# Reordered loads, unread products between the first scans, and a respread weight conversion in a fused SSD and MLP kernel

## The chip, the cores and the metric

The kernel runs on one core of a Trainium2 chip. The metric is the device time of one execution in microseconds (us). The core has a matmul engine (TensorE, PE in the tables, with its weight loads as PEld), a vector engine (VectorE, DVE), a scalar engine (ScalarE, ACT), GpSimd (POOL) and SyncE (SP), whose queue issues most of the transfers; ACT can issue transfers too. Each engine works through its own queue in order. Operands lie in SBUF, matmuls write to PSUM.

## The reference

Two stages follow each other. The first is a Mamba-2 state-space scan over 4 batches, 8 heads, 768 steps, head size 32 and state size 16. Written without its chunks of 32, with `a` clipped to 1e-6..1 and `cum` the running sum of log a:

```
L    = exp(cum[i] - cum[j]) for j <= i, else 0
y    = ((C B^T) * L) x  +  (C state) * exp(cum)
state = exp(sum log a) * state + sum_j exp(cum[-1] - cum[j]) B_j x_j
```

The second stage takes the 3072 tokens with their 8 x 32 values as 256 features:

```
h = x @ w_in            # 256 x 2048
g = h * sigmoid(1.702 h)
out = g @ w_out         # 2048 x 256
```

The weights are float64 in memory.

## The kernel before

**Tiling.** The 3072 tokens form six groups of 512 tokens. A group has two pairs `p` of 128-step chunks, so there are 12 pairs. For a group the scan stage leaves `yT`, then the hidden stage makes 16 tiles `h` (two matmuls each, over 256 features) that ACT turns into `gT` (line 402), then the projection adds up `o` over the 16 `gT`. For group 0 the projection runs in the order of the 16 blocks f (`project_all`, line 417), for the others by 128 tokens (`project`, line 410). A dictionary of places (`in_hidden[g][f]`, `in_project[g][f]`, lines 471 to 505) says which other work is written between two of these tiles. Nothing is rescheduled: `in_order` keeps each engine's instructions in the order in which the program was written.

**One pair of the scan.** `fan` (line 253): ACT copies the decay values `az` into `X`, four matmuls spread them over the partitions into PSUM `ab`. `decay_pair` (line 271): DVE makes the decay matrix `L` with four scans over `ab`. Later pairs (from 4 on) scan a tile `a` instead that a transfer has spread out of a scratch in DRAM (`spread`, line 175; `decay`, line 242). `ends` scales B to `Be`. `turn` transposes B and C (`tp`) and ACT copies them to `BT` and `CT`, DVE makes `CsT`. `scores` makes C B^T in PSUM `cb`, and DVE multiplies it into `L` (line 339). `advance` makes the new state `S` from `A` = Be^T x. `finish` adds up `y`, and ACT copies it to `yT`. `decay_rows` (line 292) clips and scans `af`, the decay values along the rows.

**Weights.** The float64 weights come as 16 pieces of 512 KB, 8 of `w_in` and 8 of `w_out`, each for two of the 16 blocks f. `fetch(i)` loads piece i as `bits`; `unpack(i)` starts with `fetch(i + AHEAD)` and then takes exponent and mantissa apart (ACT `m`, `z`, `p2`, DVE `e`, `u`); `narrow(i)` first does `unpack(i + 1)`, then three DVE steps that end in float32 weights. `bits` has AHEAD + 1 = 5 buffers, so a fetch waits until the piece five before it has been used.

**PSUM.** `h`, `o` and the first pair's `ab` share the two buffers of tag "ff"; the `ab` of other pairs shares one buffer with `cb`.

**Transfers.** All go out from SP in the order of the program, except piece 0 and x of the pairs 0 and 1, which ACT issues. Eight transfers of SP and ACT can be outstanding: each waits for the one that last used its completion counter. B and C of a pair are 64-byte runs, x 128-byte runs.

Of the kernel before, what the change touches and what calls it, by code (L numbers as in the profile page):

```python
# [8 lines left out]
FP32 = mybir.dt.float32  # L9
# [25 lines left out]
def kernel(  # L35
# [73 lines left out]
    AHEAD = 4  # L109
# [93 lines left out]

    early = const.tile([P, 1], FP32, name="early")
    nc.vector.memset(early, 0.0)
    nc.scalar.activation(early, early, AF.Silu)
    ident = const.tile([P, P], FP32, name="ident")
    make_identity(nc, ident)
    idents = const.tile([P, NH, P], FP32, name="idents")
    nc.gpsimd.tensor_copy(idents, ident.unsqueeze(1).to_broadcast([P, NH, P]))  # L210

# [5 lines left out]
    for r in range(R):  # L217
# [4 lines left out]


# [7 lines left out]
        fill=0.0, base=N - 1, channel_multiplier=-1)  # L231

# [38 lines left out]
    def decay_pair(p, ab):  # L271
# [3 lines left out]
        for r in range(R):  # L275
# [3 lines left out]
                initial=0.0, op0=ALU.mult, op1=ALU.add)  # L279

# [136 lines left out]
    def project_all(g, gT, between):  # L417
# [9 lines left out]
        for k in range(CG):  # L427
# [3 lines left out]
    nc.vector.tensor_scalar(out=az, in0=az, scalar1=1e-6, scalar2=1.0,  # L431
                            op0=ALU.max, op1=ALU.min)
    nc.vector.memset(az[:, :, 0:1], 0.0)
    for b in range(NB):
        nc.sync.dma_start(out=scratch[b].rearrange("c h s -> h c s"),
                          in_=az[b * NH:(b + 1) * NH])


    assert PG == 2
    decay_pair(0, fan(0, "ff"))  # L440
    second = fan(1, "cb")
    unpack(0)
# [4 lines left out]
    decay_pair(1, second)  # L447
    scores(0)
    advance(0)
    narrow(0)  # L450
# [8 lines left out]
    spread_rows(1)  # L459
    for p in range(PG, 2 * PG):  # L460
        load(p)
# [23 lines left out]

    for j in range(PG):
        p = PG + j
        at(in_hidden[0], 6 + 5 * j, lambda p=p: fan_at(p))
        at(in_hidden[0], 7 + 5 * j, lambda p=p: decay_at(p))
    for k, i in enumerate((8, 9, 10, 13, 14)):  # L490
        at(in_hidden[0], i, lambda k=k: narrow(NF // PF + k))
    for k, i in enumerate((2, 4, 6)):
        at(in_project[0], i, lambda k=k: narrow(NF // PF + 5 + k))
# [15 lines left out]
    for g in range(NG):  # L509
        if g + 2 < NG:  # L510
            for j in range(PG):
# [10 lines left out]
        if g + 2 < NG:  # L522
# [43 lines left out]
```

## Time and profile before

| | us |
|---|---|
| three runs, median (lowest to highest) | 457.79 (457.02 to 457.92) |
| profiled execution, time | 457.59 |
| profiled execution, span of its instructions | 455.6 |
| PE busy | 404.1 (89%) |
| DVE busy | 168.0 (37%) |
| ACT busy | 111.5 (24%) |

The span is what lies between the first and the last instruction; the execution is 2.0 us longer. Engines overlap, so busy times don't add up to the span. A busy PE is not a PE at its best rate: the clock of TensorE has two levels, 1.2 and 2.4 GHz, and the profile has a column with the granted share (0.50 or 1.00, or between where it changed inside a stretch). Work that belongs to the scan of group 0 ends at 45.0 us, its hidden stage at 103.4, its projection at 140.4, and the five other groups follow. In the rows, a matmul instruction on float32 operands shows as two records.

### The profile page before, as it was taken

How to read it: one execution, taken by the hardware profiler on the slowest of the kernel's cores; microseconds unless marked ns; L12 is line 12 of the kernel's file. 1: busy time of each engine (PE TensorE's matmuls, PEld its weight loads, DVE VectorE, ACT ScalarE, POOL GpSimd, SP SyncE). 2: the span in 40 equal slices, each digit the busy share in tenths (PEclk: the TensorE clock that was granted, in tenths of full speed). 3: DMA queues.
4: the chain of work that ended last, by engine and by line, in shares of the span. 5: the costliest groups of instructions: out<-in, count | busy, mean ns of one | idle time of the engine just before them, and what ended most of it. 6: DMA issues, size and time to landing. Idle time of an engine off the chain costs nothing.

```text
span 455.6 us, 4764 instructions
## 1 busy us (share of the span) xinstructions
PE 404.1 (89%) x1928; PEld 265.7 (58%) x1928; DVE 168.0 (37%) x227; ACT 111.5 (24%) x202; POOL 7.9 (2%) x27
## 2 busy tenths in 40 slices
PE   1547912789999999999999999999999999999996
PEld 0225300337885546885558875558855478844785
DVE  0876805977573640435051352202550300000000
ACT  3213805745202232002421012330023310033100
POOL 3000000000000000000000000000000000000000
PEclk9999975979999999999999999999999999999999
DMA  9801897260003920008600029100000000000000
GB/s 164 235 0 48 141 129 272 86 239 0 1 0 67 195 98 0 25 12 117 207 1 13 12 43 203 56 0 13 23 12 1 0 1 23 24 0 0 11 13 24
DMA packets 85973, 28.58 MB, mean 63 GB/s; under 512 B 75904, under 2 KB 79168, under 8 KB 85952
## 3 DMA queue, kind: packets, MB, share of 16 engines
q1 hardware_dynamic: 81520, 27.24, 25.4%
q10 hardware_dynamic: 4432, 1.05, 1.2%
q8 instruction: 15, 0.25, 0.2%
q14 instruction: 6, 0.05, 0.0%
HBM read 25.03 MB, written 3.24 MB: 62 GB/s over the span
## 4 chain that ended last, share of the span: by engine, by line
PE 80%; DVE 7%; SPq 5%; ACT 3%; DMA 2%; issue 2%; POOL 0%; ACTq 0%; DVEq 0%; POOLq 0%
PE h L399 31%; PE o L413 30%; PE o L424 6%; SPq L105 4%; DVE L L276 3%; PE cb L334 3%; PE y L386 3%; PE y L379 2%; PE ab L266 2%; PE A L349 2%; DMA b<-in_B_dram 1%; ACT z L146 1%; DMA bits<-in_moe_w_in_dram 1%; PE tp L313 1%; ACT p L147 1%
## 5 line engine op out<-in xcount | busy, mean ns | idle before, releaser
L399 PE MATMUL h<-yT,w_in 128*128 128x512 f32 x384 | 176.5, 605 | 2.8 <-ACT gT L402 1.5
L413 PE MATMUL o<-w_out,gT 128*128 128x256 f32 x640 | 138.9, 379 | 0.0
L413 PEld LDWEIGHTS o<-w_out,gT 128*128 128x128 f32 x640 | 121.6, 190 | 18.7 <-issue 2.4
L399 PEld LDWEIGHTS h<-yT,w_in 128*128 128x128 f32 x384 | 71.3, 192 | 86.6 <-issue 76.7
L402 ACT ACTIVATE gT<-h 128x512 f32<-128x512 f32 x96 | 57.1, 595 | 232.3 <-PE h L399 232.3
L406 DVE TENSOR_SCALAR ob<-o 128x256 f32<-128x256 f32 x24 | 10.1, 424 | 172.4 <-PE o L413 164.4
L266 PE MATMUL ab<-X,ones 32*128 32x512 f32 x32 | 11.1, 1126 | 32.4 <-ACT X L258 31.1
L248 DVE TENSOR_TENSOR_SCAN L<-a,idents 128x1024 f32<-128x1024 f32 x16 | 36.5, 2281 | 0.0
L339 DVE TENSOR_TENSOR L<-L,cb 128x2048 f32<-128x2048 f32 x12 | 27.4, 2287 | 17.6 <-PE cb L334 17.6
L424 PE MATMUL o<-w_out,gT 128*128 128x256 f32 x128 | 29.6, 383 | 0.8 <-ACT gT L402 0.8
L424 PEld LDWEIGHTS o<-w_out,gT 128*128 128x128 f32 x128 | 23.8, 190 | 5.2 <-ACT gT L402 1.2
L334 PE MATMUL cb<-CT,BT 32*128 32x256 f32 x192 | 15.6, 445 | 10.9 <-DVE L L276 7.4
L266 PEld LDWEIGHTS ab<-X,ones 32*128 32x128 f32 x32 | 3.5, 308 | 37.0 <-ACT X L258 32.8
L323 DVE TENSOR_TENSOR CsT<-tp,since 128x256 f32<-128x256 f32 (+1 forms) x12 | 4.5, 379 | 48.3 <-ACT CT L320 48.2
L276 DVE TENSOR_TENSOR_SCAN L<-ab,idents 128x512 f32<-128x512 f32 x16 | 18.4, 1204 | 10.1 <-PE ab L266 10.1
L334 PEld LDWEIGHTS cb<-CT,BT 32*128 32x128 f32 x192 | 9.8, 206 | 18.9 <-issue 14.5
L146 ACT ACTIVATE z<-e,edge 128x512 f32<-128x512 uint32 x16 | 11.5, 716 | 24.9 <-DVE e L142 24.9
L391 ACT ACTIVATE yT<-y 128x512 f32<-128x512 f32 x12 | 7.1, 595 | 30.5 <-PE y L386 30.5
L379 PEld LDWEIGHTS y<-CsT,S 128*128 128x128 f32 x80 | 11.2, 198 | 5.7 <-issue 4.5
L141 ACT ACTIVATE m<-bits 128x512 f32<-128x512 uint32 x16 | 10.7, 670 | 14.6 <-DMA bits<-in_moe_w_in_dram 13.4
L386 PE MATMUL y<-L,x 128*32 128x128 f32 x384 | 13.8, 287 | 0.0
L379 PE MATMUL y<-CsT,S 128*128 128x128 f32 x80 | 11.7, 285 | 0.9 <-DVE S L360 0.9
(47 smaller groups left out, 164.8 us busy)
## 6 DMA issues: line engine op xcount, KB each, us to landing
a<-scratch SPq DMA_DIRECT2D x16, 512.0 KB, 8.2
bits<-in_moe_w_out_dram SPq DMA_DIRECT2D x8, 512.0 KB, 3.5
bits<-in_moe_w_in_dram SPq DMA_DIRECT2D x7, 512.0 KB, 4.9
out_dram<-ob SPq DMA_DIRECT2D x24, 128.0 KB, 1.7
x<-in_x_dram SPq DMA_DIRECT2D x20, 128.0 KB, 2.9
b<-in_B_dram SPq DMA_DIRECT2D x24, 64.0 KB, 2.7
c<-in_C_dram SPq DMA_DIRECT2D x24, 64.0 KB, 2.6
af<-in_a_dram SPq DMA_DIRECT2D x4, 384.0 KB
```

What stands on the lines that cost most here:

```text
L105: queue.dma_start(out=dst[p][:, k], in_=src[b, :, sl, :].rearrange("h s d -> s h d"))
L248: nc.vector.tensor_tensor_scan(out=Ls[p][:, k].rearrange("p r q i -> p (r q i)"), data0=ra.pop(n), data1=idents.rearrange("p h i -> p (h i ...
L266: nc.tensor.matmul(out=ab[r], lhsT=ones[rows], rhs=X[rows].rearrange("p k q i -> p (k q i)"), start=True, stop=True, tile_position=(32 * r ...
L276: nc.vector.tensor_tensor_scan(out=L[:, r], data0=ab[r], data1=idents.rearrange("p h i -> p (h i)")[:, :2 * Q * P], initial=0.0, op0=ALU.m ...
L334: nc.tensor.matmul(out=cb[:, r, k], lhsT=BT[rows, k], rhs=CT[rows, k].rearrange("p q i -> p (q i)"), start=True, stop=True, tile_position= ...
L339: nc.vector.tensor_tensor(out=Lv, in0=Lv, in1=cb.rearrange("p r k e -> p k r e"), op=ALU.mult)
L379: nc.tensor.matmul(out=y[:, k, t], lhsT=old[:, t * P:(t + 1) * P], rhs=s["CsT"][:, k], start=first, stop=False, skip_group_check=True)
L386: nc.tensor.matmul(out=y[D * q:D * q + D, k, t], lhsT=rx[p][:, k, h], rhs=L[:, k, h // Q, h % Q], start=False, stop=True, tile_position=(0 ...
L399: nc.tensor.matmul(out=h, lhsT=w_in[:, k, f * P:(f + 1) * P], rhs=yT[g][:, k], start=(k == 0), stop=(k == NK - 1))
L402: nc.scalar.activation(gT, h, AF.Silu, scale=GELU_SCALE)
L413: nc.tensor.matmul(out=o, lhsT=gT[f][:, k * P:(k + 1) * P], rhs=w_out[:, f], start=(f == 0), stop=(f == NF - 1))
L424: nc.tensor.matmul(out=o[k // 2][:, k % 2], lhsT=gT[f][:, k * P:(k + 1) * P], rhs=w_out[:, f], start=(f == 0 and k % 2 == 0), stop=(f == N ...
```

## The change

- `AHEAD` is 6 and `bits` has 8 buffers. The tiles `a` of `spread` move from a ring of their own (4 buffers) into the ring of `bits`.
- The first transfers are put in another order: pieces 0 and 1 go out from SP behind `az`; then B and C of pair 0, `af`, all of pair 1, pieces 2 to 5, then all of the pairs 2 and 3, `af` of batch 1 and the scratch. ACT issues x of pair 0 alone, behind its table load. The pairs 4 and 5 and the tiles `a` of group 2 are loaded inside group 0's projection.
- POOL makes `pick` ahead of the identities. The clip of `az` is written earlier.
- `keep_busy` writes matmuls whose PSUM result `busy` is never read: three with ones ahead of the first `fan`, and one behind each of the eight scans of the pairs 0 and 1, which streams the scanned `L`.
- Piece 0 is unpacked before pair 1's `fan` and narrowed right behind pair 0's scans.
- The places in group 0: pieces 2 to 8 are narrowed in the hidden stage at f = 0, 1, 3, 4, 9, 10, 12, pieces 9 to 15 in the projection at 0, 2, 4, 6, 8, 10, 11. Before, pieces 2 to 12 were narrowed in the hidden stage and 13 to 15 in the projection. Other places shift by a few f.

```diff
-    AHEAD = 4
+    AHEAD = 6
-        bits[i] = t = wide.tile([P, 2 * PN], U32, tag="bits", name=f"bits{i}", bufs=AHEAD + 1)
+        bits[i] = t = wide.tile([P, 2 * PN], U32, tag="bits", name=f"bits{i}", bufs=AHEAD + 2)
...
-        ra[n] = raw.tile([P, NH * P], FP32, tag="a", name=f"a{n}", bufs=4)
+        ra[n] = wide.tile([P, NH * P], FP32, tag="bits", name=f"a{n}", bufs=AHEAD + 2)
...
-    fetch(0, nc.scalar)
+    fetch(0)
+    fetch(1)
+    early = const.tile([P, 1], FP32, name="early")
+    nc.vector.memset(early, 0.0)
+    nc.scalar.activation(early, early, AF.Silu)
     load(0, nc.scalar)
     spread_rows(0)
-    load(1, nc.scalar)
-    for i in range(1, AHEAD):
+    load(1)
+    for i in range(2, AHEAD):
         fetch(i)
+    for p in range(PG, 2 * PG):
+        load(p)
+    spread_rows(1)
...
+    busy = []
+    def keep_busy(rhs, n=1):
+        if not busy:
+            busy.append(ps.tile([P, 4 * P], FP32, tag="ff", name="busy"))
+        for i in range(n):
+            nc.tensor.matmul(out=busy[0], lhsT=ones, rhs=rhs, start=True, stop=True,
+                             skip_group_check=True)
...
-    def decay_pair(p, ab):
+    def decay_pair(p, ab, after=None):
...
+            if after:
+                after(L[:, r])
...
-    decay_pair(0, fan(0, "ff"))
+    keep_busy(ones.unsqueeze(1).to_broadcast([P, 4, P]), 3)
+    ab = fan(0, "ff")
+    unpack(0)
     second = fan(1, "cb")
-    unpack(0)
+    busy.clear()
+    decay_pair(0, ab, keep_busy)
+    narrow(0)
     decay_rows(0)
...
-    decay_pair(1, second)
+    decay_pair(1, second, keep_busy)
     scores(0)
     advance(0)
-    narrow(0)
     turn(1)
...
-    spread_rows(1)
-    for p in range(PG, 2 * PG):
-        load(p)
...
+    for i, k in zip((2, 3, 4, 5, 6, 7, 8), (0, 1, 3, 4, 9, 10, 12)):
+        at(in_hidden[0], k, lambda i=i: narrow(i))
+    for p, k in ((PG, 5), (PG + 1, 13)):
+        at(in_hidden[0], k, lambda p=p: fan_at(p))
+        at(in_hidden[0], k + 1, lambda p=p: decay_at(p))
+    for i, k in zip(range(9, 16), (0, 2, 4, 6, 8, 10, 11)):
+        at(in_project[0], k, lambda i=i: narrow(i))
+    for k in range(CG):
+        at(in_project[0], 3 + 2 * k, lambda k=k: spread(2 * CG + k))
+    for k in range(PG):
+        at(in_project[0], 4 + 4 * k, lambda k=k: load(2 * PG + k))
```

SP, from piece 6 on, before. The names are destination and source of a transfer (`bits6` is piece 6, `b2` is B of pair 2).

```order
L126 DMA bits6_291<-in_moe_w_in_dram 128x2x512
L186 DMA af1_328<-in_a_dram 128x1x768
L105 DMA b2_330<-in_B_dram 128x8x16 x2
L105 DMA c2_331<-in_C_dram 128x8x16 x2
L105 DMA x2_332<-in_x_dram 128x8x32 x2
L105 DMA b3_339<-in_B_dram 128x8x16 x2
L105 DMA c3_340<-in_C_dram 128x8x16 x2
L105 DMA x3_341<-in_x_dram 128x8x32 x2
L105 DMA b4_348<-in_B_dram 128x8x16 x2
L105 DMA c4_349<-in_C_dram 128x8x16 x2
L105 DMA x4_350<-in_x_dram 128x8x32 x2
```

B, C and x of pair 5 follow, and only then piece 7. SP, the same stretch now, from piece 5 on (`bits_116`; `bits_183`, `bits_213` and `bits_328` are the pieces 6, 7 and 8, `b_118` and `b_127` B of the pairs 2 and 3):

```order
L126 DMA bits_116<-in_moe_w_in_dram 128x2x512
L105 DMA b_118<-in_B_dram 128x8x16 x2
L105 DMA c_119<-in_C_dram 128x8x16 x2
L105 DMA x_120<-in_x_dram 128x8x32 x2
L105 DMA b_127<-in_B_dram 128x8x16 x2
L105 DMA c_128<-in_C_dram 128x8x16 x2
L105 DMA x_129<-in_x_dram 128x8x32 x2
L186 DMA af_136<-in_a_dram 128x1x768
L241 DMA scratch<-az 8x6x128 x4
L126 DMA bits_183<-in_moe_w_in_dram 128x2x512
L126 DMA bits_213<-in_moe_w_in_dram 128x2x512
L126 DMA bits_328<-in_moe_w_out_dram 128x2x512
```

Piece 7 stood behind 24 transfers of B, C and x that were issued after piece 6; now nothing stands between the two, and 12 such transfers and the scratch stand ahead of both.

PE in the first scans, before (`ab` of the pairs 0 and 1, the transposes `tp`, then `cb` and `A` of pair 0):

```order
L266 MATMUL ab_163<-X_160,ones 128x512 x4
L313 MATMUL tp_187<-ident,b_85 128x128 x2
L313 MATMUL tp_187<-ident,c_86 128x128 x2
L334 MATMUL cb_207<-CT_194,BT_192 128x256 x8
L349 MATMUL A_217<-x_87,Be_199 128x256 x2
```

And now:

```order
L278 MATMUL ab_198<-X_195,ones 128x512 x4
L290 MATMUL busy<-L_203,ones 128x512 x4
L337 MATMUL tp_235<-ident,b_90 128x128 x2
L337 MATMUL tp_235<-ident,c_91 128x128 x2
L290 MATMUL busy<-L_250,ones 128x512 x4
L358 MATMUL cb_259<-CT_242,BT_240 128x256 x8
L373 MATMUL A_269<-x_92,Be_247 128x256 x2
```

Four unread products stand ahead of the transposes of pair 0, four more ahead of its `cb`; each waits for its scan on DVE.

DVE between the scans of pair 0 and those of pair 1, before:

```order
L276 SCALAR_TENSOR_TENSOR L_155<-ab_3_150,idents 128x512
L142 TENSOR_SCALAR e_170<-bits_83 128x512
L148 TENSOR_SCALAR u_171<-bits_83 128x512
L295 TENSOR_SCALAR af_94<-af_94 128x768
L302 SCALAR_TENSOR_TENSOR since_185<-af_94,first_181 128x768
L323 TENSOR_TENSOR CsT_197<-tp_187,since_185 128x128
L286 TENSOR_TENSOR Be_199<-b_85,L_155 128x128 x2
L276 SCALAR_TENSOR_TENSOR L_202<-ab_163,idents 128x512 x4
```

And now:

```order
L298 SCALAR_TENSOR_TENSOR L_203<-ab_3_178,idents 128x512
L142 TENSOR_SCALAR e_215<-bits_85 128x512
L148 TENSOR_SCALAR u_216<-bits_85 128x512
L159 SCALAR_TENSOR_TENSOR m_187<-u_186,m_187 128x512
L161 SCALAR_TENSOR_TENSOR p_189<-bits_83,p_189 128x512
L167 TENSOR_TENSOR w_in<-m_187,p_189 128x2x256
L319 TENSOR_SCALAR af_99<-af_99 128x768
L326 SCALAR_TENSOR_TENSOR since_233<-af_99,first_229 128x768
L347 TENSOR_TENSOR CsT_245<-tp_235,since_233 128x128
L310 TENSOR_TENSOR Be_247<-b_90,L_203 128x128 x2
L298 SCALAR_TENSOR_TENSOR L_250<-ab_198,idents 128x512 x4
```

The whole of `narrow(0)`, with the unpacking of piece 1, now stands in front of `decay_rows`; the two steps on piece 0 went ahead of pair 0's scans, and the five steps leave the place behind pair 0's new state.

## Rows read from the trace of the kernel before

**Rows 1.** Stages: length, busy time per engine, granted clock, transfer share, GB/s

```profile
core 0: us, PE busy (x) PEld busy (x) DVE busy (x) ACT busy (x) POOL busy (x), PEclk, DMA share, GB/s
45.00:103.40 58.40, 35.55 (x84) 14.06 (x85) 37.04 (x66) 29.48 (x51) 0.00 (x0) 0.80 0.70 169
103.40:140.40 37.00, 36.17 (x249) 30.05 (x246) 24.00 (x32) 9.24 (x17) 1.04 (x3) 1.00 0.00 0
140.40:455.60 315.20, 311.18 (x1458) 208.88 (x1458) 80.03 (x89) 60.56 (x112) 1.34 (x5) 1.00 0.19 43
```

**Rows 2.** Timeline, the stall: start, us, engine, line, tiles, [idle before <- releaser]

```profile
45.62 1.93 SPq L105 DMA_DIRECT2D b<-in_B_dram  x2
...
66.52 0.53 SPq L126 DMA_DIRECT2D bits<-in_moe_w_in_dram  x1
...
70.67 0.43 DVE L142 TENSOR_SCALAR e<-bits 128x512 uint32<-128x512 uint32 x1 [13.96 <-DMA bits<-in_moe_w_in_dram]
...
76.77 2.09 PE L266 MATMUL ab<-X,ones 32*128 32x512 f32 x8 [17.45 <-ACT X L258]
```

**Rows 3.** Chain that ended last, up to 45 us: start, us, what

```profile
0.80 2.64 DMA az<-in_a_dram
...
7.76 0.57 DVE az L431
...
9.49 2.13 PE ab L266 x4
...
14.99 2.34 DVE L L276 x2
...
22.60 3.44 DVE L L276 x3
...
26.17 2.12 PE cb L334 x16
...
28.32 2.29 DVE L L339
...
31.25 0.48 DVE S L360
...
34.69 2.09 PE cb L334 x16
...
40.82 0.70 DVE S L353
```

**Rows 4.** The same chain, a later group's hidden stage

```profile
396.77 27.47 PE h L399 x64
```

**Rows 5.** Timeline at the start of group 0's hidden stage

```profile
45.00 7.13 PE L399 MATMUL h<-yT,w_in 128*128 128x512 f32 x16 [1.19 <-ACT yT L391]
...
49.44 0.58 ACT L402 ACTIVATE gT<-h 128x512 f32<-128x512 f32 x1
...
51.87 0.58 ACT L402 ACTIVATE gT<-h 128x512 f32<-128x512 f32 x1
```

**Rows 6.** The same timeline later, up to the second fan

```profile
86.54 0.42 DVE L142 TENSOR_SCALAR e<-bits 128x512 uint32<-128x512 uint32 x1
...
89.14 0.42 DVE L142 TENSOR_SCALAR e<-bits 128x512 uint32<-128x512 uint32 x1
...
91.20 0.58 ACT L402 ACTIVATE gT<-h 128x512 f32<-128x512 f32 x1
...
92.62 2.09 PE L266 MATMUL ab<-X,ones 32*128 32x512 f32 x8 [4.16 <-ACT X L258]
```

**Rows 7.** Stretches of 1 us around the clock's changes, columns as in rows 1

```profile
63.00:64.00 1.00, 0.00 (x0) 0.00 (x0) 0.00 (x0) 0.00 (x0) 0.00 (x0) 0.71 1.11 157
80.00:81.00 1.00, 1.00 (x3) 0.34 (x2) 1.00 (x2) 0.00 (x0) 0.00 (x0) 0.76 0.00 0
90.00:91.00 1.00, 0.00 (x0) 0.00 (x0) 1.00 (x2) 0.97 (x2) 0.00 (x0) 0.86 0.92 348
97.00:98.00 1.00, 1.00 (x3) 0.40 (x2) 1.00 (x2) 0.00 (x0) 0.00 (x0) 0.72 1.02 389
```

More of the change, by code (lines that the diff above doesn't have):

```diff
@@ L202 @@
     nc.vector.memset(edge[:, 1:2], float(255 << 23))
[L204 to L210, printed above, removed]
     ones = const.tile([P, P], FP32, name="ones")
@@ L221 @@
                                 channel_multiplier=1)
+    ident = const.tile([P, P], FP32, name="ident")
+    make_identity(nc, ident)
+    idents = const.tile([P, NH, P], FP32, name="idents")
+    nc.gpsimd.tensor_copy(idents, ident.unsqueeze(1).to_broadcast([P, NH, P]))
     same = const.tile([P, NH, D], FP32, name="same")
@@ L231 @@
         fill=0.0, base=N - 1, channel_multiplier=-1)
+    nc.vector.tensor_scalar(out=az, in0=az, scalar1=1e-6, scalar2=1.0,
+                            op0=ALU.max, op1=ALU.min)
+    nc.vector.memset(az[:, :, 0:1], 0.0)
+    for b in range(NB):
+        nc.sync.dma_start(out=scratch[b].rearrange("c h s -> h c s"),
+                          in_=az[b * NH:(b + 1) * NH])
     part = const.tile([P, Q], FP32, name="part")
@@ L428, in project_all @@
             store(g, k, o[k // 2][:, k % 2])
[L431 to L436, printed above, removed]
     assert PG == 2
-    decay_pair(0, fan(0, "ff"))
+    keep_busy(ones.unsqueeze(1).to_broadcast([P, 4, P]), 3)
+    ab = fan(0, "ff")
+    unpack(0)
     second = fan(1, "cb")
-    unpack(0)
+    busy.clear()
+    decay_pair(0, ab, keep_busy)
+    narrow(0)
     decay_rows(0)
@@ L472 @@
     in_project = [{} for _ in range(NG)]
-    done = 2
-    for i in range(done, NF // PF):
-        at(in_hidden[0], i - done, lambda i=i: narrow(i))
     wait = {}
@@ L484, in decay_at @@
         ends(p, 1)
-    for j in range(PG):
[L487 to L493, printed above, removed]
+    for i, k in zip((2, 3, 4, 5, 6, 7, 8), (0, 1, 3, 4, 9, 10, 12)):
[5 more added lines that the diff above has]
+        at(in_project[0], k, lambda i=i: narrow(i))
+    for j in range(PG):
+        scan_at(in_project[0], PG + j, [6 * j + i for i in (1, 2, 3, 6)])
+    at(in_project[0], 5, lambda: decay_rows(1))
+    for k in range(CG):
+        at(in_project[0], 3 + 2 * k, lambda k=k: spread(2 * CG + k))
+    for k in range(PG):
+        at(in_project[0], 4 + 4 * k, lambda k=k: load(2 * PG + k))
     for k in range(2):
-        at(in_project[0], 10 + 4 * k, lambda k=k: decay(2 * CG + k))
+        at(in_project[0], 13 + k, lambda k=k: decay(2 * CG + k))
         at(in_hidden[1], 4 + 2 * k, lambda k=k: decay(2 * CG + 2 + k))
-    for j in range(PG):
-        scan_at(in_project[0], PG + j, [8 * j + i for i in (0, 1, 3, 6)])
-    at(in_project[0], 5, lambda: decay_rows(1))
     for g in range(1, NG - 1):
@@ L510 @@
         if g + 2 < NG:
-            for j in range(PG):
+            for j in range(PG if g else 0):
                 load((g + 2) * PG + j)
@@ L521 @@
                 do()
-        if g + 2 < NG:
+        if 0 < g < NG - 2:
             for n in range(*bring[g]):
```

## The prediction

> **What bounds the kernel now.** First the busy times by stage [rows 1]. From 140.4 us on PE is busy 311 of 315 us at the full clock, and in group 0's projection 36.2 of 37.0. No edit shortens a matmul there, so those 315 us stay. What is left is the 45 us of the first scans and the 58.4 us of group 0's hidden stage, where PE works 35.6 us at a mean clock of 0.80. A later group's 64 matmul records of that stage take 27.47 us [rows 4]: 0.43 each, 1.72 for one of the 16 h.
>
> Then the timeline of that stage, to see what PE waits for [rows 2]. SP begins on the 24 transfers of B, C and x at 45.6 and comes to piece 7 only at 66.5; it lands at 70.67, after DVE has sat idle for 14 us. Behind it stand, on ACT, a gT and the X of the fan, so PE is idle for 17.45 us. The second fan waits 4.16 us, for ACT [rows 6]. Then the chain of waits up to 45 us [rows 3]: it runs through the arrival of `az`, the eight scans on DVE and the small matmuls between them. Those run at the lower of the two levels (1.2 GHz): the first `ab` takes 2.13 us, as at 76.77 where the granted clock is half [rows 2, 3], though the clock column shows 1.00 before 45 us. I go by durations there.
>
> The sum is made against the profiled execution: 457.6 us, 2.0 more than its span and 0.2 below the median of the runs, which is taken as no difference.
>
> **The first scans, part by part.**
> Arrival of `az`. DVE starts its clip at 7.76, ab at 9.49 [rows 3]. The four transfers are issued by about 2.6, and the first landed in 2.64, so the last could land at 5.2. Before, piece 0 and three transfers of x went out from ACT beside them; now x comes behind ACT's table load and the pieces behind `az` in SP's queue. I take 5.2: −2.55 us. If nothing changes it is 0.
> A rule stands against that term. The Trainium skill, "DMA: Bandwidth & Descriptors", section "Issuing engines are not separate DMA queues", says that transfers run on the same 16 engines and interleave whichever engine started them. By that rule alone piece 0 would slow `az` from SP as it did from ACT, the term would be 0 and the time 432.8; the rows of before, with both at once, cannot tell.
>
> Scans of pair 0. They end at 17.33, 7.84 after ab starts [rows 3]. The three products with ones (two records each, 0.86 us at the full rate, 1.72 at half) fill PE from 1.2 to about 6, when nothing else could run. If they raise the clock, ab takes 1.06, the third ab no longer delays DVE, and the scans take 0.66 for the two unpacking steps of piece 0 that now stand ahead, then 4 x 1.15 [rows 3]: ab at 6.93, end at 13.4, 6.47 after: −1.4. At half rate it is about +0.1. I take −1.4.
>
> Between the pairs. `narrow(0)` now stands here. One conversion is 2.60 us of DVE (86.54 to 89.14 [rows 6]); 0.66 of unpacking leaves: +1.95. Pair 1's scans then end at 24.05, not 26.04.
>
> The unread products of pair 1. They are not free: `cb` of pair 0 is queued behind the fourth on PE, and DVE's product waits for `cb`. The first can start after one scan, at 20.6, after an idle PE of more than 4 us. The clock fell 2.2 us after the last matmul at 88.5 and 4.1 us after that at 59.3, and rose 3.7 and 4.9 us after work began [rows 2, 5, 6, 7]. So they start at half rate, and end at 25.9 if it rises after 3.7, 26.5 after 4.9, 27.5 if not at all. I take 26.2: cb starts 2.15 later than the scans would allow, and takes half of its 2.12: +1.1.
>
> Behind S of pair 0. It ends at 31.73, and pair 1's product on DVE starts only at 36.8, behind cb at 34.69 + 2.1 [rows 3], because the conversion stands between. Without it DVE has only CsT and Be, 0.85 us, and cb of pair 1, at the full rate, is done in their cover: −4.25. Without that clock it is −3.2.
>
> Behind that product. It ends at 36.8 + 2.29 = 39.1, and S starts at 40.82 [rows 3], since y and A, 4.0 us at half rate, came late. At the full rate they take about 2, which the product hides: −1.7, else 0.
>
> Sum: −2.55 − 1.4 + 1.95 + 1.1 − 4.25 − 1.7 = −6.85. The hidden stage starts at 38.1, not 45.0.
>
> **The hidden stage.** What goes is the wait for piece 7: it is asked for in the first scans, 9 us ahead of use (below). Late next is ACT: a gT behind a conversion's three steps comes 2.43 us after the last (49.44, 51.87 [rows 5]), PE needs 1.72, and "ff" has two buffers. Counting from the first h, the order is that of before up to gT of f = 2 at 6.87. Conversions stand now at f = 0, 1, 3, 4, so h of f = 4 waits 0.65. ACT then has two conversions, and gT of f = 5 starts at 12.35; ab starts 1.42 behind its gT (91.20 to 92.62 [rows 6]), at 13.8. PE ended at 10.95: idle 2.8. By the same steps the conversions at 9, 10 and 12 cost 0.65, and the fan at 13 idles PE for 2.05. Both ab take 1.06 at the full rate. Sum: 27.5 + 2.8 + 2.05 + 2.1 + 1.3 = 35.75.
> An idle time of 2.8 us lies between the 2.2 and 4.1 after which the clock fell. A fall costs 1.05 on ab and, from 1.7 to 2.9 us at half rate behind it, about 1.15: 2.2. I take one fall, at the first fan: 37.9. Before, from 45.0 to the first o at 103.4: 58.4. −20.5.
>
> **The projection.** It gets four more whole conversions than its three: 10.4 us. DVE was busy 24.0 of 37.0 us [rows 1]; 34.4 still fits, and counted step by step every piece is ready 0.2 to 1.5 us before its o (the closest are f = 8 and 12). The scans end 1 us earlier in it, the ob copies wait about 1 us behind the two `decay` scans that are now last. I take 0; bounds −1 and +3. The tiles `a` and the loads of the pairs 4 and 5 go out here, where the transfers are idle (share 0.00 [rows 1]), ten or more us before their use.
>
> Total: −6.85 − 20.5 = −27.35, so 430.2.
>
> **The rivals.**
> The clock helps less. Every small matmul of the chain up to cb at 34.69, still 2.09, ran at half rate [rows 3], though PE had had work since 9.5, so the unread products may not lift them. Then the terms are −2.55 + 0.1 + 1.95 + 2.4 (products to 27.5, with `ab` late as well, and cb at half) − 3.2 + 0: the hidden stage at 43.7, and the second fan falls too, +2.2: 438.
> The clock never falls in the hidden stage: −2.2, 428; with `az` earlier or the products ending at 25.9, 426 to 427. For it: PE kept its clock over the 1.19 us idle at 45.0 [rows 5]. Against it: one fall 2.2 us after a last matmul.
> DVE becomes the bound of the projection. If a conversion takes 2.9 in place of 2.6 there, by overlaps lost, seven cost 2.1, and the covers of 0.2 are gone: 433.
> Pieces 6 and 7 are late, so the wait is not removed but moved. Ahead of them in SP's queue stand 24 transfers of B, C and x, at 20.9 us for 24 [rows 2], six pieces and ten others. Pieces at 4.15 each from issue to landing (66.52 to 70.67 [rows 2]), none overlapping, would be 25, the others 5: 51 + 4 to land, where use is at 47. That is 8 late, 438. With overlap, as eight may be outstanding, they land at about 40.
> Slower than before takes the same queue at twice that length: piece 6 not there before 47 + 27 = 75 us. Each us behind 47 costs one, so at 80 us it is 463. Nothing but a doubling of the 0.87 us per small transfer speaks for it.
>
> **How the numbers follow.** Forecast as written, 426.5 to 434 with the bounds of its terms: 0.52. Clock helping less, 434 to 440: 0.20. No fall, 424 to 428: 0.12. DVE bound, 433: 0.08. Pieces late, 433 to 445: 0.05. Slower, 463: 0.02; the gains lost entirely, 457: 0.01. The range takes in the forecast, the case without a fall, DVE's and most of the clock's: 425 to 439. A measurement of this kernel can tell 0.2% (0.9 us) from no change. Faster 0.97, same 0.01, slower 0.02.
>
> **What would show it.** The first h at 37 to 39 us; ab behind the first products at 1.06 against 2.1; the fourth product on pair 1 ending 2 us after its scan; no DVE wait for a piece behind 40 us; PE idle 2.8 and 2 us at the fans, and a granted clock of 0.50 behind the first; from the first o to group 1 37 us; from there 315. A first h at 43 or an o that waits for a conversion would make the forecast wrong.

## The result, and the profile after

The changed kernel takes 431.9 us (median of four runs, 431.06 to 434.07), the kernel before beside it 457.4: a ratio of 0.9457, with a 95% interval from 0.9412 to 0.9501. The forecast was 430.2 with a range of 425 to 439. The profiled execution of the changed kernel took 434.07 us, with a span of 432.2; it is the slowest of its four runs, 2.2 above their median. That of before took 457.6. All stages below come from these two executions.

| stage | before | forecast | measured |
|---|---|---|---|
| start to the first `h` | 45.0 | 38.1 | 43.3 |
| first `h` to first `o` (hidden stage) | 58.4 | 37.9 | 37.4 |
| first `o` to group 1 (projection) | 37.0 | 37.0 | 36.5 |
| group 1 to the last instruction | 315.2 | 315 | 315.05 |

The stages of the changed kernel by windows, with the columns of [rows 1]:

```profile
43.30:80.70 37.40, 32.50 (x81) 13.18 (x82) 26.89 (x46) 22.85 (x40) 0.00 (x0) 0.95 0.47 127
80.70:117.10 36.40, 36.37 (x251) 30.17 (x249) 34.53 (x53) 16.07 (x27) 1.24 (x3) 1.00 0.25 59
117.10:432.20 315.10, 311.18 (x1458) 208.87 (x1458) 80.17 (x89) 60.55 (x112) 1.35 (x5) 1.00 0.18 43
```

Beside [rows 1], PE is busy for 32.5 us of the hidden stage in place of 35.55, at a mean granted clock of 0.95 in place of 0.80, and the stage lost 21 us. DVE's work went from the hidden stage (37.0 to 26.9 us) to the projection (24.0 to 34.5), which stayed as long as PE needs. The last window did not move.

Nearly the whole gain is in the hidden stage. The first scans, for which most of the new instructions were written, gave 1.7 us where 6.85 were forecast. The timeline of PE and DVE up to the first `h` shows why (start, us, engine, line, tiles, idle before and what ended it):

```profile
1.21 5.49 PE L290 MATMUL busy<-ones 128*128 128x512 f32 x6 [1.21 <-DVE ones L212]
7.46 1.13 PE L278 MATMUL ab<-X,ones 32*128 32x512 f32 x4 [0.77 <-ACT X L270]
9.90 4.89 PE L278 MATMUL ab<-X,ones 32*128 32x512 f32 x12 [1.31 <-DVE L L298]
14.72 6.58 PE L290 MATMUL busy<-L,ones 128*128 128x512 f32 x8
21.14 0.38 PE L337 MATMUL tp<-ident,b 128*128 128x128 f32 x2
24.80 6.66 PE L290 MATMUL busy<-L,ones 128*128 128x512 f32 x8 [3.06 <-DVE L L298]
31.39 1.15 PE L358 MATMUL cb<-CT,BT 32*128 32x256 f32 x16
43.31 7.13 PE L423 MATMUL h<-yT,w_in 128*128 128x512 f32 x16 [1.19 <-ACT yT L415]
```

```profile
5.72 0.56 DVE L237 TENSOR_SCALAR az<-az 128x768 f32<-128x768 f32 x1 [4.57 <-DMA az<-in_a_dram]
22.92 0.29 DVE L347 TENSOR_TENSOR CsT<-tp,since 128x128 f32<-128x128 f32 x1 [3.23 <-ACT CT L344]
23.53 4.56 DVE L298 TENSOR_TENSOR_SCAN L<-ab,idents 128x512 f32<-128x512 f32 x4
32.60 2.29 DVE L363 TENSOR_TENSOR L<-L,cb 128x2048 f32<-128x2048 f32 x1 [4.51 <-PE cb L358]
36.85 2.29 DVE L363 TENSOR_TENSOR L<-L,cb 128x2048 f32<-128x2048 f32 x1
```

The unread products (`busy`, line 290) hold PE twice. The four on pair 0's scans run from 14.72 to 21.3, and the transposes `tp` stand behind them; DVE waits 3.23 us for what ACT makes of these. The four on pair 1's scans hold `cb` until 31.39, though those scans end at 28.09, and DVE waits 4.51 us. What the clock does beside them, in stretches of 1 us (columns as in [rows 1], granted clock third from the end):

```profile
10.00:11.00 1.00, 1.00 (x2) 0.19 (x2) 0.96 (x1) 1.00 (x3) 0.00 (x0) 0.65 0.97 91
20.00:21.00 1.00, 1.00 (x3) 0.48 (x2) 0.00 (x0) 0.00 (x0) 0.48 (x1) 0.73 1.00 360
30.00:31.00 1.00, 1.00 (x3) 0.33 (x1) 0.00 (x0) 0.00 (x0) 0.00 (x0) 0.61 1.06 116
58.00:59.00 1.00, 1.00 (x5) 0.48 (x2) 0.83 (x1) 0.00 (x0) 0.00 (x0) 0.54 0.00 0
```

It fell shortly after 10, rose about 20.5, fell again while PE waited for pair 1's first scan (0.50 from 24 on), and rose only near 30.8, when pair 1's products had nearly ended. Both groups of products ran mostly at the lower level (1.2 GHz). The last row is the one fall in the hidden stage, just behind the first fan.

In the hidden stage the wait for piece 7 [rows 2] is gone. The pieces 6 and 7 go out together from SP at 35.36, 8 us before the first `h`, and no instruction of DVE waits for a piece after 40 us. What is left there are the two fans:

```profile
35.36 0.91 SPq L126 DMA_DIRECT2D bits<-in_moe_w_in_dram  x2
56.96 1.14 PE L278 MATMUL ab<-X,ones 32*128 32x512 f32 x8 [2.45 <-ACT X L270]
76.07 1.14 PE L278 MATMUL ab<-X,ones 32*128 32x512 f32 x8 [1.71 <-ACT X L270]
```

Idle times of 2.45 and 1.71 us stand where [rows 2, 6] had 17.45 and 4.16, and each `ab` runs at the full rate, 1.14 in place of 2.09.

### The profile page after: what moved, and what is told of

It is laid out like the page before. It is cut to its first block, busy times and chain, and to the rows that moved or that the text cites. A ratio compares the mean times of both kernels' runs of the same rounds, so it can differ in the third digit from the quotient of the medians.

```text
span 432.2 us, 4810 instructions
## 1 busy us (share of the span) xinstructions
PE 413.8 (96%) x1950; PEld 268.1 (62%) x1950; DVE 168.5 (39%) x227; ACT 112.0 (26%) x202; POOL 8.1 (2%) x27
## 4 chain that ended last, share of the span: by engine, by line
PE 89%; ACT 5%; DVE 3%; DMA 1%; issue 1%; SPq 0%; ACTq 0%; DVEq 0%
PE h L423 36%; PE o L437 32%; PE o L448 7%; PE busy L290 3%; PE cb L358 3%; PE y L410 2%; PE ab L278 2%; PE y L403 2%; PE A L373 2%; ACT z L146 1%; ACT gT L426 1%; DVE L L363 1%; PE tp L337 1%; ACT m L141 1%; ACT p L147 1%; DMA az<-in_a_dram 1%
## 5 line engine op out<-in xcount | busy, mean ns | idle before, releaser
L260 DVE TENSOR_TENSOR_SCAN L<-a,idents 128x1024 f32<-128x1024 f32 x16 | 36.5, 2282 | 0.0
L290 PE MATMUL busy<-L,ones 128*128 128x512 f32 x16 | 13.2, 1002 | 3.1 <-DVE L L298 3.1
L358 PE MATMUL cb<-CT,BT 32*128 32x256 f32 x192 | 13.7, 400 | 1.2 <-ACT CT L344 1.2
L358 PEld LDWEIGHTS cb<-CT,BT 32*128 32x128 f32 x192 | 8.7, 184 | 9.4 <-issue 7.0
L278 PE MATMUL ab<-X,ones 32*128 32x512 f32 x32 | 8.3, 804 | 6.2 <-ACT X L270 4.9
L290 PEld LDWEIGHTS busy<-L,ones 128*128 128x128 f32 x16 | 5.0, 326 | 11.1 <-issue 5.1
L147 ACT ACTIVATE p<-z,edge 128x512 uint32<-128x512 f32 x16 | 11.6, 722 | 0.5
```

The lines of the kernel that those rows point to most:

```text
L260: nc.vector.tensor_tensor_scan(out=Ls[p][:, k].rearrange("p r q i -> p (r q i)"), data0=ra.pop(n), data1=idents.rearrange("p h i -> p (h i ...
L278: nc.tensor.matmul(out=ab[r], lhsT=ones[rows], rhs=X[rows].rearrange("p k q i -> p (k q i)"), start=True, stop=True, tile_position=(32 * r ...
L290: nc.tensor.matmul(out=busy[0], lhsT=ones, rhs=rhs, start=True, stop=True, skip_group_check=True)
L358: nc.tensor.matmul(out=cb[:, r, k], lhsT=BT[rows, k], rhs=CT[rows, k].rearrange("p q i -> p (q i)"), start=True, stop=True, tile_position= ...
```

## The experiments

The question was which part brings how much, and what the unread products are worth, since the trace showed them delaying what they were to speed up. Nine kernels, and the change once more, were run, each in four runs beside the kernel before on the same chip (three chips in all; the kernel before had medians of 457.73, 457.79 and 457.78 on them). Theory A is in each case the reading of the traces seen up to then.

| kernel | median us | range | ratio to before, 95% interval | `az` clip | first `h` | hidden stage |
|---|---|---|---|---|---|---|
| the change | 431.9 | 431.06 to 434.07 | 0.9412 to 0.9501 | 5.72 | 43.3 | 37.4 |
| without the products | 431.36 | 431.01 to 432.44 | 0.9405 to 0.9436 | 6.05 | 40.05 | 39.0 |
| products of pair 1 alone | 431.82 | 430.43 to 432.16 | 0.9408 to 0.9447 | 6.46 | 39.9 | 39.0 |
| old loads | 435.79 | 435.5 to 436.91 | 0.9507 to 0.9542 | 8.30 | 43.9 | 38.7 |
| before with the new loads | 442.07 | 441.58 to 442.53 | 0.9641 to 0.9672 | 6.23 | 44.0 | 44.7 |
| old places of the conversion | 438.12 | 437.64 to 441.57 | 0.9551 to 0.9631 | 6.08 | 40.7 | 43.0 |
| first loads from ACT | 436.11 | 434.92 to 437.24 | 0.9505 to 0.9569 | 7.89 | 44.4 | 37.3 |
| products put elsewhere | 428.03 | 427.21 to 429.74 | 0.9330 to 0.9388 | 6.38 | 38.1 | 37.3 |
| the same, and at the fans | 426.66 | 425.2 to 428.31 | 0.9290 to 0.9360 | 5.78 | 36.2 | 35.7 |
| products at the fans alone | 429.35 | 429.13 to 429.55 | 0.9367 to 0.9412 | 6.21 | 40.4 | 35.6 |
| the change again | 434.49 | 432.28 to 434.91 | 0.9452 to 0.9531 | 5.93 | 42.0 | 38.8 |

The last three columns are of each kernel's profiled execution, in us; they differ between executions of one kernel, as the first and the last row show.

**No products at all.** The three calls are dropped:

```diff
-    keep_busy(ones.unsqueeze(1).to_broadcast([P, 4, P]), 3)
...
-    busy.clear()
-    decay_pair(0, ab, keep_busy)
+    decay_pair(0, ab)
...
-    decay_pair(1, second, keep_busy)
+    decay_pair(1, second)
```

> The changed kernel without any of its eleven unread products. Theory A (the products delay what is queued behind them on PE about as much as the clock they bring is worth): in the changed kernel CsT waits 3.2 us behind pair 0's products and cb 3.2 us behind pair 1's; without them those 6.4 us go, but the small matmuls stay at half rate (scans of pair 0 about 1 us later, cb 1.0, A 1.0 to 1.7 and so on, together 5 to 6). First h at 42 to 43 us instead of 43.3, time 430 to 433. Rival B (the clock is worth more than the wait): first h at 45 or later, time 434 or more. A third way, that the products cost clearly more than they bring: first h below 41, time below 429.

It measured 431.36, 0.5 below the change, which its runs can't tell from no difference. The time is theory A's, but the first `h`, at 40.05, is that of the third way. The timeline of PE and DVE:

```profile
26.40 2.09 PE L358 MATMUL cb<-CT,BT 32*128 32x256 f32 x16 [9.30 <-DVE L L298]
30.18 0.38 PE L337 MATMUL tp<-ident,b 128*128 128x128 f32 x2
40.05 7.13 PE L423 MATMUL h<-yT,w_in 128*128 128x512 f32 x16 [1.19 <-ACT yT L415]
```

```profile
21.09 0.29 DVE L347 TENSOR_TENSOR CsT<-tp,since 128x128 f32<-128x128 f32 x1
```

`CsT` waits for nothing, and `cb` starts as soon as pair 1's scans are done; it runs at half rate, 2.09, but it is done at 28.5, and the changed kernel's at 32.5. `tp` of pair 1 is at the full rate again at 30.18, with no product to lift it. So the first `h` comes 3.3 us earlier. The hidden stage then takes 1.6 longer, because the clock fell at both fans (windows, columns as in [rows 1]):

```profile
54.00:56.00 2.00, 2.00 (x9) 0.50 (x5) 0.34 (x1) 0.00 (x0) 0.00 (x0) 0.50 0.00 0
74.00:76.00 2.00, 2.00 (x3) 0.76 (x4) 2.00 (x2) 0.00 (x0) 0.00 (x0) 0.61 0.77 77
```

So the products cost the first scans 3.3 us between these two profiles, and 1.9 against the second profile of the change (last run below), where the first `h` is at 42.0. That they bring nothing on the whole holds for the placing of the change.

**Products of pair 1 alone.** `decay_pair(0, ab, keep_busy)` becomes `decay_pair(0, ab)`; the three ahead of the first `fan` and the four of pair 1 stay.

> The changed kernel without the four products behind pair 0's scans; the three with ones and the four behind pair 1's scans stay. Theory A: the transposes of pair 0 start at about 15 instead of 21.1 and CsT no longer waits, so all behind it comes 3.2 us earlier: first h at about 40, time 428 to 430. Rival B (pair 0's products keep the clock up for what follows, so what is won on CsT is lost on slower products of pair 1): pair 1's four products still end 3 us or more behind the last scan and cb stays late; first h at 42 to 44, time 431 to 434.

```profile
22.48 5.54 PE L290 MATMUL busy<-L,ones 128*128 128x512 f32 x8 [5.86 <-DVE L L298]
27.95 1.15 PE L358 MATMUL cb<-CT,BT 32*128 32x256 f32 x16
```

On the timeline `CsT` now starts at 20.60 without a wait, and the first `h` comes 3.4 earlier than in the change, as theory A had it. `cb` still waits behind its four products, 2.2 us behind the scans' end at 25.8. The time, 431.82, lies in the rival's range, though not by the late first `h` that it named: here too the clock fell at both fans (0.50 from 54 to 56 us and from 74 to 76), and the hidden stage gave 1.6 back. So the wait of `CsT` is due to pair 0's products; the theory lacked what the clock does later.

**Old loads.** The change with the loads of before: AHEAD 4, 5 buffers of `bits`, a ring of its own for `a`, and the old order of transfers:

```diff
-    fetch(0)
-    fetch(1)
+    fetch(0, nc.scalar)
+    load(0, nc.scalar)
+    spread_rows(0)
+    load(1, nc.scalar)
+    for i in range(1, AHEAD):
+        fetch(i)
     early = const.tile([P, 1], FP32, name="early")
     nc.vector.memset(early, 0.0)
     nc.scalar.activation(early, early, AF.Silu)
-    load(0, nc.scalar)
-    spread_rows(0)
-    load(1)
-    for i in range(2, AHEAD):
-        fetch(i)
-    for p in range(PG, 2 * PG):
-        load(p)
-    spread_rows(1)
...
+    spread_rows(1)
+    for p in range(PG, 2 * PG):
+        load(p)
```

The loads of the pairs 4 and 5 and the tiles `a` also go back to where they were.

> The changed kernel with the loads as they were before (order, five buffers, own ring for the tiles a, pairs 4 and 5 ahead of piece 7); products and new places stay. Theory A (the loads remove a wait, but the new places alone would hide most of it, since piece 7 is now unpacked at f = 9 and not at f = 4): piece 7 lands at about 69 us, ACT wants it at about 67 to 69, so the hidden stage grows by 2 to 4 us, and az comes 2 us later: time 434 to 439. Rival B (the order of the loads carries most of the gain): the wait for piece 7 comes back with 10 us or more of idle PE, time 442 to 450.

435.79, 3.9 above the change's first four runs and in theory A's range. The timeline of SP, DVE and PE:

```profile
64.01 0.58 SPq L126 DMA_DIRECT2D bits<-in_moe_w_in_dram  x1
68.98 0.43 DVE L142 TENSOR_SCALAR e<-bits 128x512 uint32<-128x512 uint32 x1 [5.13 <-DMA bits<-in_moe_w_in_dram]
71.82 1.96 PE L417 MATMUL h<-yT,w_in 128*128 128x512 f32 x4 [2.63 <-DVE w_in L167]
```

Piece 7 is nearly as late as in [rows 2] (68.98 against 70.67), but with the conversions spread out DVE comes to it only at 63.9, not at 56.7: DVE waits 5.1 us and PE 2.6, in place of 14 and 17.45. The new places alone take away most of the big wait, and the hidden stage is 1.3 us longer than in the change, not 2 to 4. What the later loads add in the time, once the new places are there, this run does not show: it also has the first loads issued from ACT, and that alone measured 436.11 (below). How far ahead pieces are fetched, the shared ring and the order were not tried one by one.

**Before with the new loads.** The other half: the kernel before with AHEAD 6, the shared ring and the new order of transfers, without products and with the old places.

```diff
-    AHEAD = 4
+    AHEAD = 6
...
-    fetch(0, nc.scalar)
+    fetch(0)
+    fetch(1)
...
-    load(1, nc.scalar)
-    for i in range(1, AHEAD):
+    load(1)
+    for i in range(2, AHEAD):
         fetch(i)
+    for p in range(PG, 2 * PG):
+        load(p)
+    spread_rows(1)
```

> The kernel before with the new loads alone (order, eight buffers shared with the tiles a, pairs 4 and 5 and the tiles a inside the projection); no products, old places of the conversions and scans. Theory A: the wait of 14 us for piece 7 goes, but one conversion per f keeps ACT ahead of PE by nothing: the hidden stage takes about 45 us instead of 58.4, and az lands up to 2 us earlier: time 441 to 445. Rival B (the loads carry nearly all of the gain): hidden stage 38 to 40, time 433 to 437.

442.07, 10.2 above the change, as theory A had it. The hidden stage takes 44.7 in place of 58.4; its windows row and its fans:

```profile
44.00:88.70 44.70, 36.21 (x84) 14.45 (x85) 37.74 (x67) 29.08 (x51) 0.00 (x0) 0.89 0.58 152
```

```profile
61.98 1.14 PE L269 MATMUL ab<-X,ones 32*128 32x512 f32 x8 [3.67 <-ACT X L261]
77.15 2.09 PE L269 MATMUL ab<-X,ones 32*128 32x512 f32 x8 [3.59 <-ACT X L261]
```

The loads alone take away the wait for the piece. What is late is ACT and DVE: in the first blocks a `gT` comes every 2.42 us, as in [rows 5], since each stands behind a conversion, and the fans idle PE for 3.6 us each. With the new places the hidden stage is 7.4 us shorter, most of the 8.4 us between the two profiled executions.

**Old places of the conversion.** The changed kernel with the places of before: pieces 2 to 12 narrowed in the hidden stage, 13 to 15 in the projection, fans at f = 6 and 11.

```diff
-    for i, k in zip((2, 3, 4, 5, 6, 7, 8), (0, 1, 3, 4, 9, 10, 12)):
-        at(in_hidden[0], k, lambda i=i: narrow(i))
+    for i in range(2, NF // PF):
+        at(in_hidden[0], i - 2, lambda i=i: narrow(i))
...
+        at(in_hidden[0], 6 + 5 * j, lambda p=p: fan_at(p))
+        at(in_hidden[0], 7 + 5 * j, lambda p=p: decay_at(p))
...
+    for k, i in enumerate((8, 9, 10, 13, 14)):
+        at(in_hidden[0], i, lambda k=k: narrow(NF // PF + k))
```

> The changed kernel with the old places in group 0 (pieces 2 to 12 narrowed in the hidden stage, one per f at first; fans at f = 6 and 11); new loads and products stay. Theory A (ACT is what is late next, a gT every 2.43 us where conversions stand at each f): the hidden stage takes 43 to 46 us instead of 37.4, the projection is not shorter, being bound by PE: time 438 to 441. Rival B (once piece 7 is there, the places matter little): hidden stage 38 to 40, time 432 to 435.

438.12, 6.2 above the change and in theory A's range. The windows row and the fans on the timeline:

```profile
40.70:83.70 43.00, 33.39 (x84) 13.24 (x85) 36.68 (x66) 29.33 (x50) 0.00 (x0) 0.96 0.60 157
```

```profile
58.67 1.14 PE L278 MATMUL ab<-X,ones 32*128 32x512 f32 x8 [3.64 <-ACT X L270]
73.58 1.75 PE L278 MATMUL ab<-X,ones 32*128 32x512 f32 x8 [4.18 <-ACT X L270]
```

The hidden stage is 5.6 us longer than in the change, with 9.8 us more of DVE's work in it. Moving that work into the projection costs nothing there: 37.15 us with the old places, 36.48 with the new. The conversions, the fans and the later steps of the scans went back together, so this run does not say which of their places matters most.

**First loads from ACT.** The changed kernel, with piece 0 and x of the pairs 0 and 1 issued from ACT as before, and all else of the change kept:

```diff
-    fetch(0)
+    fetch(0, nc.scalar)
     fetch(1)
+    load(0, nc.scalar)
...
-    load(0, nc.scalar)
...
-    load(1)
+    load(1, nc.scalar)
```

> The changed kernel with piece 0 and x of the pairs 0 and 1 issued by ACT ahead of its table load, as before. Theory A (what goes out beside az from ACT slows its arrival): az is clipped at about 7.7 us instead of 5.7, and all behind it comes 2 us later unless the clock changes with it: time 433 to 435. Rival B (transfers share the engines whoever issues them): az is clipped at 5.5 to 6.2, time 431 to 433.

```profile
0.80 0.44 ACTq L126 DMA_DIRECT2D bits<-in_moe_w_in_dram  x1
7.89 0.56 DVE L237 TENSOR_SCALAR az<-az 128x768 f32<-128x768 f32 x1 [6.74 <-DMA az<-in_a_dram]
```

436.11, 4.2 above the change and above both ranges. The clip of `az` starts at 7.89 on the timeline, 2.2 later; in the eight kernels that issue piece 0 from SP it starts between 5.72 and 6.46, in this one and in the one with the old loads at 7.89 and 8.30. That issuing them from ACT as before delays `az` is shown, as theory A had it. But piece 0 then also goes out earlier, at 0.80 beside `az`, where SP issues it at 2.71, behind the last `az`; whether the queue or the moment does it was not tried apart. Its price in the time is less sure: the first `h` is 1.1 us later by the profiles, the hidden stage is the same, and the change's own two sets of runs (below) have medians 2.6 apart.

**Products put elsewhere.** If a product is worth having and only stands in the wrong place, it has to stand where PE has nothing behind it that DVE waits for. Pair 0's products go behind the transposes of pair 0 and read `ones`, so that they need not wait for scans; pair 1 loses its last one, and a product is put between the second and the third `ab` of pair 0. `busy` gets a PSUM buffer of the tag "sm".

```diff
         for r in range(R):
+            if p == 0 and r == 2:
+                keep_busy(ones.unsqueeze(1).to_broadcast([P, 4, P]))
...
-            if after:
+            if after and r < R - 1:
...
-    busy.clear()
-    decay_pair(0, ab, keep_busy)
+    decay_pair(0, ab)
     narrow(0)
     decay_rows(0)
     turn(0)
+    keep_busy(ones.unsqueeze(1).to_broadcast([P, 4, P]), 8)
```

> The changed kernel with its products where nothing waits behind them: after the first three, one between the second and third ab, none behind pair 0's scans, eight with ones behind the transposes of pair 0, three behind pair 1's first three scans. Theory A (order on PE costs 6.4 us, the clock itself is worth its price): clock mostly at the upper level from 5 us on, CsT and cb wait for nothing, first h at 36 to 38, time 424 to 427. Rival B (these matmuls do not hold the clock): the products run at half rate, cb late by 1 to 3 us, first h at 39 to 42, time 428 to 432.

```profile
9.18 2.04 PE L292 MATMUL busy<-ones 128*128 128x512 f32 x2
14.55 7.03 PE L292 MATMUL busy<-ones 128*128 128x512 f32 x16
26.17 1.15 PE L360 MATMUL cb<-CT,BT 32*128 32x256 f32 x16
38.09 7.13 PE L425 MATMUL h<-yT,w_in 128*128 128x512 f32 x16 [1.19 <-ACT yT L417]
```

The eight products run at the full rate, 0.44 a record, behind the transposes; `cb` starts right behind pair 1's scans and takes 1.15. The one between the `ab` does not: the clock had fallen at 9.2 us and came back at 12.7. The first `h` is at 38.1, where the forecast had put it, and the time is 428.03, 3.9 below the change. Both lie a little above what theory A gave, the time at the lower end of the rival's range; by the trace the mechanism is theory A's, `CsT` and `cb` waiting for no product.

**The same, and at the fans.** Two more products ahead of each later `fan`, where PE waits for ACT:

```diff
     def fan_at(p):
+        busy.clear()
+        keep_busy(ones.unsqueeze(1).to_broadcast([P, 4, P]), 2)
         wait[p] = fan(p, "cb")
```

> The kernel of the run before (products where nothing waits) with two more products with ones ahead of each of the two fans of group 0's hidden stage, where PE is idle for 2.4 and 1.7 us in the changed kernel and the granted clock fell to one half at 58.5 for 3 us. Theory A: the clock stays up through the hidden stage, which then takes 35.5 to 36.5 us instead of 37.4: 1 to 2 us faster than the run before. Rival B: the products, 0.86 us each, delay ab by as much as they win, no difference within 0.7 us.

```profile
47.19 1.88 PE L292 MATMUL busy<-ones 128*128 128x512 f32 x4
49.79 1.14 PE L280 MATMUL ab<-X,ones 32*128 32x512 f32 x8 [0.72 <-ACT X L270]
```

```profile
36.20:71.80 35.60, 34.15 (x88) 14.04 (x89) 26.82 (x46) 22.85 (x40) 0.00 (x0) 1.00 0.62 187
```

426.66, the fastest of all, 5.2 us below the change and 1.4 below the run before, as theory A had it. The two products fill 1.9 of the 2.45 us for which PE waited at the fan, nothing comes later by them, and the granted clock is 1.00 through the whole stage, which takes 35.7. The first `h`, at 36.2, comes 1.9 us before that of the run before, though the instructions up to it are the same: this profile is of the fastest of the kernel's four runs, and the clock did not fall near 9 us in it.

**Products at the fans alone.** The kernel without products, with those two lines in `fan_at` and `busy` in the tag "sm".

> The changed kernel without its eleven products, but with two products with ones ahead of each fan of group 0's hidden stage. Theory A (the products pay where PE would stand idle ahead of a fan, and hardly in the first scans): first h at 40 to 41 as without products, hidden stage 35.5 to 36.5 as in the run with fans, so 427 to 429, within 2 us of the run that has both. Rival B (the products in the first scans are what holds the clock later on): the clock falls in the hidden stage all the same, hidden stage 37 to 39, time 430 to 432.

```profile
40.40:76.00 35.60, 34.17 (x88) 14.07 (x89) 26.83 (x45) 22.82 (x40) 0.00 (x0) 1.00 0.48 134
```

429.35: 2.0 below the kernel without products, with the hidden stage at 35.6 and the clock at 1.00 again, as in the run before this. Theory A was right on the stage and on the first `h`, and wrong in leaving the products of the first scans next to nothing: it had this run within 2 us of the one that has both, and it is 2.7 above. The two runs together price both places: the products at the fans are worth 2.0 us without the others and 1.4 with them (there the ranges overlap), those in the first scans, well placed, 2.7 (429.35 to 426.66).

**The change again.** The changed kernel as it is, to see which of its waits come back.

> The changed kernel once more, to see how far the place where the clock rises moves from one execution to the next. Theory A (its first profile shows a late first h of 43.3 because the clock rose only 6 us into pair 1's products, which is not the same each time): another first h, 39 to 43, with the same wait of CsT behind pair 0's products; time 431 to 433. Rival B (the 43.3 us are fixed by the order): first h at 43.0 to 43.6 again.

```profile
7.67 2.08 PE L278 MATMUL ab<-X,ones 32*128 32x512 f32 x4 [2.23 <-ACT X L270]
25.66 4.47 PE L290 MATMUL busy<-L,ones 128*128 128x512 f32 x8 [3.06 <-DVE L L298]
30.05 1.15 PE L358 MATMUL cb<-CT,BT 32*128 32x256 f32 x16
```

```profile
23.78 0.29 DVE L347 TENSOR_TENSOR CsT<-tp,since 128x128 f32<-128x128 f32 x1 [2.95 <-ACT CT L344]
```

The clock behind the wait for pair 1's first scan, in the change's first profile and in this one (columns as in [rows 1]):

```profile
25.00:30.00 5.00, 5.00 (x6) 1.92 (x7) 3.08 (x3) 0.00 (x0) 0.00 (x0) 0.50 0.82 100
26.00:31.00 5.00, 5.00 (x24) 1.61 (x22) 2.95 (x3) 0.00 (x0) 0.00 (x0) 1.00 1.04 119
```

The wait of `CsT`, 2.95 us, and the hold of `cb` come back: they are the order's. The clock's moments do not. The first `ab` ran at half rate this time, 2.08. Ahead of pair 1's products PE waited 3.06 us for the scan in both executions, and the clock fell in the first and not in this one: granted 0.50 from 25 to 30 us there, 1.00 from 26 to 31 here, so that the four products ended at 30.1, 1.1 us behind the scans. The first `h` is at 42.0, as theory A had it, and the hidden stage takes 38.8, with the same sum to 0.1 us. The time is outside theory A's range: the median, 434.49, is 2.6 above that of the first four runs, with ranges that overlap; all eight lie between 431.06 and 434.91. A difference to the change of less than 2.6 us is therefore not read as one above.

## Why the prediction was right, and where it was not

The time fell into the range 1.7 us above the forecast, and the mechanism was the right one: the wait for piece 7 and what ACT and DVE were late with in the hidden stage. By its own steps:

- *Hidden stage, −20.5.* Measured −21.1 by the profiles. The fans idle PE for 2.45 and 1.71 us, forecast 2.8 and 2.05; there was one fall of the clock, at the first fan, as written. That it was one is luck: in the seven profiles with idle times of 2.4 and 1.7 us at the fans it fell once in four, twice in two (the kernels without products and with those of pair 1 alone), and nowhere in the one with the old loads (mean granted clock 1.00).
- *Projection, 0.* Measured −0.5. DVE is busy for 34.5 us, forecast 34.4, and no `o` waits long enough to matter: PE is busy 36.37 of 36.40 us. The rival of a DVE that becomes the bound is out.
- *Pieces 6 and 7.* Issued at 35.4; DVE waits for none after 40 us. The rivals of late pieces are out, the slower one with them. Two numbers in them were off, without weight for the result: SP's queue has 22 transfers of B, C and x ahead of the two pieces, not 24, as x of pair 0 goes out from ACT; and the slower rival's 47 + 27 is 74, and the 80 us that it then goes by is not derived.
- *Arrival of `az`, −2.55.* Measured −2.04. The rule of the Trainium skill, "DMA: Bandwidth & Descriptors", section "Issuing engines are not separate DMA queues", that transfers interleave on the same 16 engines whichever engine started them, was weighed against this term. The run with the first loads from ACT shows what issuing them there, beside `az`, costs: a clip 2.2 us later, which fits shared engines. But what was drawn from the rule, that pieces behind `az` in SP's own queue slow it as much, did not come true in any run: the clip starts between 5.72 and 6.46 there, and at 7.76 to 8.30 in the three kernels with piece 0 from ACT. The median lies beside the 432.8 that stood for that case, for other reasons: the term came, and the next one failed.
- *Scans of pair 0, −1.4.* Measured −0.96: they start 2.0 us earlier by `az` and end 3.0 earlier than in [rows 3]. The first `ab` ran at the full rate (1.13), but the clock had fallen by the third, which DVE waited 0.68 us for, 1.05 before. In the second profile the first `ab` ran at half rate and the term is 0: the scans end 7.83 us after `ab` starts, 7.84 before. So the three products ahead did not bring this term each time.
- *The unread products, +1.1.* This is the step that failed, in two ways. The prediction priced only those of pair 1. The four on pair 0's scans it did not price at all, though the order shows them ahead of the transposes: the conversion grows by 1.95 as forecast, but pair 1's scans end 5.05 us further behind pair 0's than before, and the other 3.1 is the wait of `CsT`. Pair 1's own hold `cb` for 3.3 us, not 2.15, because the clock rose 6.0 us after they began and the prediction took 3.7 to 4.9 from rows; in the second profile it had not fallen, and they hold it for 1.1. With `cb` at 1.15 in place of 2.12 that is +2.2 net here. Both together: +5.3 in place of +1.1. The kernel without products has neither, and its first `h` is 3.3 us earlier.
- *Behind S, −4.25 and −1.7.* The second product on DVE starts 1.97 us behind the first one's end, which was 6.2 before: −4.2. `S` starts right behind it: −1.7. The sizes are right, but not what the prediction made of them without the unread products' clock, −3.2 and 0. Two kernels without any products show that the conversion's leaving did nearly all of this. Where it stayed (before with the new loads, first two rows) the gap is 6.2 and `S` waits 2.2; where it left (the kernel without products, last two) the gap is 2.4 and `S` waits 0.4:

```profile
35.33 2.29 DVE L342 TENSOR_TENSOR L<-L,cb 128x2048 f32<-128x2048 f32 x1 [1.35 <-PE cb L337]
39.81 0.69 DVE L356 TENSOR_TENSOR S<-A,same 128x512 f32<-128x512 f32 x1 [2.20 <-PE A L352]
33.20 2.29 DVE L363 TENSOR_TENSOR L<-L,cb 128x2048 f32<-128x2048 f32 x1 [0.41 <-PE cb L358]
35.88 0.69 DVE L377 TENSOR_TENSOR S<-A,same 128x512 f32<-128x512 f32 x1 [0.39 <-PE A L373]
```

Worked out, −2.04 − 0.96 + 1.95 + 3.1 + 2.2 − 4.2 − 1.7 is −1.7: the first `h` at 43.3. The forecast named this number: a first `h` at 43 would make it wrong, and there it was wrong, by 5.2 us. Half a us each from the hidden stage and the projection, and the 2.2 us by which the profiled execution lies above the median, hide most of that in the time. So that the time lies only 1.7 us from the forecast is in part luck; the second set of runs lies 4.3 above it, still in the range. The rival "the clock helps less" had 43.7 and 438; it had the right place for the first `h`, but by other causes: a late `ab`, which only the second profile shows, and an `S` that comes no earlier and a second fall at the fans, which neither shows.

What is not settled is what decides whether the clock falls at an idle time of 1.7 to 3.1 us, and with it 1 to 2 us of an execution. That the two products at the fans keep it at 1.00 was seen in the profile of both kernels that have them, and the kernel with products at the fans alone has a mean clock of 0.999 or 1.000 in all four runs. Of the kernel with products everywhere two runs, 427.8 and 428.3, show 0.987 and 0.988: there the clock fell somewhere, and no trace shows whether at the fans or in the first scans.

## What to carry to other kernels

A transfer's place in the queue of the engine that issues it is part of the schedule: order loads by first use, and spread the work that needs them as well, since each of the two alone left PE idle, by 2.6 us for a piece or by 7.3 at the fans. Work that is written only to hold the clock is not free on its own engine; put it behind everything that another engine waits for, and into waits that are there anyway, and price each instruction queued behind it. Here, against the kernel without products, it was worth nothing that could be measured as first placed, 3.3 us when moved, and 4.7 with the products at the fans.

## What was not expected of the hardware

The granted clock fell shortly after 10 us in the changed kernel, 3.6 us after the last of the first products ended (6.70), though PE had run two small `ab` (four records) from 7.46 to 8.6 at the full rate in between and was running others. With one more full product at 8.57 in the fastest kernel's profile it did not fall; but in the kernel with the products put elsewhere, which has the same instructions up to there, it fell at 9.2, as that product began, after PE had been idle for 1.80 us ahead of `ab` in place of 0.82. So the one product does not decide it. Of two executions of the same kernel, with PE idle for 3.06 us at the same place, the clock fell in one and stayed in the other; where it fell, it came back 6.0 us after the products began, longer than the 3.7 and 4.9 of before; with the products of pair 1 alone it took 3.7. And before the first change that the trace records, the clock column shows 1.00 while the matmuls run at half rate: in the kernel without products the first `ab` takes 2.08 under a column of 1.00, so durations decide there.
